# A second buffer for Strassen's raw weights, and spectral rows split in place, in a state-space and feed-forward kernel

## The chip, the core and the metric

The kernel runs on one core of a Trainium2 chip. Five engines work side by side, each through its own instructions in order, and wait for each other by semaphores: TensorE (PE in the profile, its weight loads PEld) multiplies, VectorE (DVE) and ScalarE (ACT) work on elements, GpSimd (POOL) and SyncE (SP) here mostly issue transfers. Transfers between the device's memory and the core's on-chip memory run on 16 shared DMA engines; an issue stands in the queue of the engine that makes it, and what comes behind it in that queue waits as long as it does.

The metric is the time of one execution in device microseconds. A run gives one such time; a profiled run gives also the span, from its first to its last instruction.

## What is computed

Three terms are added up: the input u (2048 x 576), a state-space convolution of the normalised input, and a feed-forward block of it with SiLU between two matrices (576 x 4608 and 4608 x 576), all in fp32.

```python
xn = _layernorm(x, axis=-1)
return x + _A_ref(xn, A_A_re, ..., A_Dskip) + _B_ref(xn, B_w1, B_w2)

def _A_ref(u, ...):                  # u is xn here
    K = einsum("dn,dnl,dn->dl", Cc, exp(logdA[:, :, None] * l), dB).real
    y = irfft(rfft(pad(u)) * rfft(pad(K)))[:L]     # along the 2048 positions
    return y + u * Dskip

def _B_ref(x, w1, w2):
    return einsum("bsf,fd->bsd", silu(einsum("bsd,df->bsf", x, w1)), w2)
```

## The kernel before

**Numbers in two parts.** Products run in fp32r, a rounded fp32. Each operand is split into a high part h (a cast on ACT) and a low part l = value - h (a subtraction on DVE), and a product is the sum of three matmuls: h by h, h by l, l by h. Splits of this kind are the commonest work of ACT and DVE: `split_w1` and `split` for w1, `split_of` (L985 the cast, L986 the subtraction) for spectral rows.

**The feed-forward part** is the main sequence (`ffn`). 2048 positions are four blocks of 512, two halves of two. w1 and w2 are cut along 4608 into 36 tiles of 128, nine chunks of four. `up` makes a 128 x 512 tile of the hidden layer (L298 to L300), with SiLU and split behind it (L306 to L308); `down` multiplies hidden tiles with w2 (L328) and adds the result into `acc` on DVE (L333). The first half and two chunks of the second half are done so. The other seven chunks of the second half, 28 tiles of 128, are done by `wino_ffn` as 14 *units* n = 4 to 17 of two tiles each, by Strassen's scheme: seven products of 256 x 256 by 512 positions (p1, p5, p6, p7, c11, c12, c2x; L453 and L459) in place of eight.

**Raw weights.** For each unit `load_w1` fetches a 576 x 256 piece of w1 from memory into a tile `w1r` of 5 x 256 numbers in each of the 128 partitions: three transfers on SP's queue (L244 to L246). `prep` then works on the tile in five steps, spread over the iteration of the unit before: the splits "c2" and "c1" (L370 the cast, L371 the subtraction), "sums" (L381 to L384, in place), and the splits "t13" and "t24". A split's results, `w1h` and `w1l`, are what PE multiplies. The tile w1r is in a pool with one buffer (`wp`), so a unit can be fetched only when the last split of the one before, its t24, has read the tile. The call for unit n+2 stands at the end of iteration n, where t24 of unit n+1 has just been put in line. The last unit, 17, is left out of that row: `tail` asks for it, into a pool of the tail (`yp`) that lies where the spectral tiles were.

**The w2 tiles of these units** come from a buffer in memory where their parts were stored before (L482, POOL's queue, tile w).

**The convolution** is the side sequence (`side`), woven into the main one by `weave`, step for step. `kgen` makes the kernel K from tables (L795 to L897), `spread` makes the first stage of the transform of u; both leave rows in memory, d1u and d1k. `spectral` then runs 32 steps k. A step fetches a row block of each (`raw`, L935, tiles ur and kr, one buffer each, SP's queue), splits both (`split_of`, L985 and L986, tiles uh, ul, kh, kl, two buffers each), multiplies them with transform matrices (L994, banks pu and pk), multiplies the two spectra on ACT and DVE (L920 to L929), and in its second part splits the result y, transforms it (pb, L994) and copies it out (L952) to d2 (L953, POOL's queue). All three banks come from one pool of three PSUM buffers, so a product has to wait until ACT's copies (L920 to L923, L952) or DVE's products have emptied the bank used three products before. ur and kr are used again as soon as their split is done; uh and ul when PE is through with the step two before.

**The tail** (`tail`) fetches d2 (L1001, tiles ys) and makes the last transform (L1013), which is added into the output.

**The order** of instructions on each engine is fixed when the program is built: a scheduler takes them in the order of the text, with priorities, and places each by a simulated time line. `issue_after` (through `behind`) keeps one behind another.

Of the kernel before, what the change touches and what calls it, by code (L numbers as in the profile page):

```python
# [10 lines left out]
F32 = mybir.dt.float32  # L11
# [6 lines left out]
P = 128  # L18
L = 2048
D = 576  # L20
# [21 lines left out]
def kernel(  # L42
# [186 lines left out]
    def ffn():  # L229
# [4 lines left out]
        R1, R2 = {}, {}  # L234
        begun = {}

        def load_w1(half, c, t, pool=None):

            f = c * FT + t
            first = half == 0 and c == 0  # L240
            r1 = (pool or (pa if first and t else w1x if t and w1x else wp)).tile([P, 5, 2 * P], F32, tag="w1r", name="w1r", bufs=1)
            fs = slice(f * P, (f + 2) * P)
            eng = nc.gpsimd if first and t == 0 else nc.sync
            eng.dma_start(r1[:, 0:4, :], w1[0:512, fs].rearrange("(k p) f -> p k f", p=P))  # L244
            eng.dma_start(r1[0:64, 4, :], w1[512:576, fs])
            pins["load"] = eng.dma_start(r1[64:128, 4, :], w1[512:576, fs]).ins  # L246
            R1[half, c, t] = r1
# [188 lines left out]
    def wino_ffn(load_w1, prep, WT, first, end, W2, before, down):  # L436

        ps_a = ps1.tile([P, 512], F32, tag="ps1", name="pa")
        ps_c = ps1.tile([P, 512], F32, tag="ps1", name="pc")
        A, A22, S1, S2, S3, S4, x40, x41, d4 = wino["x"]  # L440
        nc.tensor.matmul(ps_a, x40[:, :P], x40, start=True, stop=True)
        G = {}

        def unit(name, n, a):
            h, l = WT[name, n]
            return h[:, a:a + 2], l[:, a:a + 2]

        def prod(dst, w, x, start=False, stop=False):
            (wh, wl), (xh, xl) = w, x
            n = 0  # L450
            for a, v in ((wh, xh), (wh, xl), (wl, xh)):
                for kt in range(2):
                    pins["pe"] = nc.tensor.matmul(dst, a[:, kt], v[:, kt], start=start and n == 0, stop=stop and n == 5,  # L453
                                                  skip_group_check=True).ins
                    n += 1

        def rest(dst, name, n, at, x4, stop=True):
            for i in range(2):
                pins["pe"] = nc.tensor.matmul(dst, WT[name, n][i][:, at], x4, start=False, stop=stop and i == 1,  # L459
                                              skip_group_check=True).ins  # L460

        def gate(src, b, f):
            gf = gp.tile([P, 512], F32, tag="gf", name="gf", bufs=2)
            spare = len(G) % 6 == 5
            gh, gl = ((wino["pool"] if spare else gp).tile([P, 512], F32R, tag=n, name=n) for n in ("gh", "gl"))
            G[b, f] = gh, gl
            with tc.high_priority():
                nc.scalar.activation(gf, src, AF.Silu)
                pins["gh"] = nc.scalar.copy(gh, gf).ins  # L469
                pins["gl"] = nc.vector.tensor_sub(gl, gf, gh).ins  # L470

        def load(n):
            if n < end - 1:
                load_w1(1, n // 2, n % 2 * 2)

        wino["last"] = lambda pool: load_w1(1, (end - 1) // 2, (end - 1) % 2 * 2, pool)

        def second(n, i):
            if n < end:
                f = 2 * n + i  # L480
                w = wp.tile([P, 2, D], F32R, tag="w2", name="w2", bufs=FT + 1)
                pins["load"] = nc.gpsimd.dma_start(w, dw2[f - WINO_C * FT]).ins  # L482
                W2[1, f // FT, f % FT] = w

        load(first + 1)
        second(first, 0)

        def downs(n):

            if n < first:  # L490
                return [lambda jj=jj: down(before, jj) for jj in range(4)]
            b = 1 - n % 2
            if n == first:
                ns = (n,)
            else:
                ns = (n - 1, n)
            return run_of(b, ns)

        def run_of(b, ns):
            fs = [2 * n + i for n in ns for i in range(2)]  # L500
            blk = (1, NCH - 1 if ns[-1] == end - 1 else WINO_C, b)
            return [lambda jj=jj: down(blk, jj, [(G[b, f], W2[1, f // FT, f % FT]) for f in fs]) for jj in range(4)]

        for n in range(first, end):
            d = downs(n - 1)
            pb = ps2.tile([P, 512], F32, tag="ps2", name="pb2")
            f5 = wino["pool"].tile([P, 512], F32, tag="f5", name="f5", bufs=1)
            units = {k: unit(*k) for k in (("c1", n, 0), ("c1", n, 2), ("t13", n, 0), ("t13", n, 2),
                                           ("t24", n, 0), ("t24", n, 2), ("c2", n, 0))}

            def p1():
                prod(pb, units["c1", n, 0], A[0], start=True)
                with tc.high_priority():
                    nc.scalar.copy(ps_a, pb)

            def p5():
                prod(ps_c, units["t13", n, 0], S1, start=True)
                rest(ps_c, "c2", n, 2, x41)
                with tc.high_priority():
                    nc.scalar.copy(f5, ps_c)  # L520

            def p6():
                prod(pb, units["t24", n, 0], S2)
                with tc.high_priority():
                    nc.vector.tensor_add(ps_c, pb, f5)

            def p7():
                prod(pb, units["t13", n, 2], S3)
                with tc.high_priority():
                    nc.vector.tensor_add(f5, pb, f5)  # L530

            def c11():
                prod(ps_a, units["c1", n, 2], A[1])
                rest(ps_a, "c1", n, 4, x40)
                gate(ps_a, 1, 2 * n)

            def c12():
                prod(ps_c, units["c2", n, 0], S4)
                rest(ps_c, "c2", n, 2, d4)
                gate(ps_c, 1, 2 * n + 1)  # L540

            def c2x():
                gate(f5, 0, 2 * n + 1)
                prod(pb, units["t24", n, 2], A22)
                gate(pb, 0, 2 * n)

            def c1x():
                c12()
                c11()

            def side_w(k):
                if k == 1:
                    prep(n + 1, "c2")
                elif k == 2:
                    prep(n + 1, "c1")
                    prep(n + 1, "sums")
                elif k == 3:
                    second(n, 1)
                    second(n + 1, 0)

            if n == first:
                order = ((p1, 0), (c11, 1), (2,), (p5, p6, 3), (p7,))
                ends = c12, c2x
            else:
                order = ((p1, p5), (0,), (p6, 1), (p7, 2), (3,))
                ends = (c1x, c2x) if n % 2 == 0 else (c2x, c1x)
            for steps in order:
                for f in steps:
                    if callable(f):
                        f()  # L570
                    else:
                        d[f]()
                        side_w(f)
                yield 0
            rest(pb, "c1", n, 4, x41, stop=False)
            for k, f in enumerate(ends):
                f()
                prep(n + 1, ("t13", "t24")[k])
                yield 0
            load(n + 2)  # L580
        b = 1 - (end - 1) % 2
        for f in run_of(b, (end - 2, end - 1)):
            f()
            yield 0
        for k, f in enumerate(run_of(1 - b, (end - 1,))):
            f()
            if k % 2:
                yield 0
# [311 lines left out]
    def spectral():  # L900
# [5 lines left out]
        def front(k):  # L906
            m3 = mats("m3", k, 2)
            m2 = m2s.pop(k)
            if k < 31:
                m2s[k + 1] = mats("m2", k + 1, 0)  # L910
            us, ks = (split_of(t, n) for t, n in zip(raws.pop(k), "uk"))
            if k < 31:
                raws[k + 1] = raw(k + 1)
            ka = kl.tile([P, D], F32, tag="ka", name="ka", bufs=2)
# [15 lines left out]
            return m3, ka  # L930

        def raw(k):
            t = [kl.tile([P, D], F32, tag=n + "r", name=n + "r") for n in "uk"]
            for r, d in zip(t, (d1u, d1k)):
                nc.sync.dma_start(r, d[k * P:(k + 1) * P, :])  # L935
            return t

        m2s = {0: mats("m2", 0, 0)}
# [19 lines left out]
    def tail():  # L958
# [9 lines left out]
                conv_load(j + i + AHEAD)  # L968
            store(y, j, (nc.gpsimd,), accum_op=ALU.add)

        with behind(pins["load"]):
            wino["last"](yp)
        steps = [(tail_at[0] + j * tail_at[1], conv_load, j) for j in range(AHEAD)]
        steps += [(tail_at[2] + j * tail_at[3], last, j) for j in range(0, 8, 2)]
        for at, f, j in sorted(steps, key=lambda v: v[0]):
# [2 lines left out]
                f(j)  # L978

    yss = {}  # L980

    def split_of(t, tag, bufs=2):
        h = kl.tile([P, D], F32R, tag=tag + "h", name=tag + "h", bufs=bufs)
# [38 lines left out]
    def side():  # L1022
# [38 lines left out]
        s4 = s4p.tile([P, 32], F32, name="s4")  # L1061
        nc.gpsimd.dma_start(s4, cs4)

        xp = ctx.enter_context(tc.tile_pool(name="xp", bufs=1))
        with tc.tile_pool(name="sx", bufs=1) as sx:
            for k, _ in enumerate(wino_x(sx, xp)):
# [95 lines left out]
```

## Time and profile before

| | us |
|---|---|
| median of 3 runs | 1121.45 (1119.86 to 1123.09) |
| the profiled run's own time | 1121.59 |
| its span, first to last instruction | 1119.7 |
| busy: PE, DVE, ACT, POOL | 1091.6, 950.0, 728.1, 140.5 |
| TensorE clock granted | 1.00 all through |

Lines of the profile give, for a group, its line in the kernel, engine, operation, and tiles as output<-inputs. In order of time a row gives start, duration, engine, line, operation, tiles, count, and in brackets the idle time of that engine just before and what ended it. Rows of waits give who waited for whom, the total in us, how often, and the longest. SPq is SP's queue of transfers. The matmuls' ends are modelled, so a busy PE is not PE at its peak.

### The profile page before, as it was taken

How to read it: one execution, taken by the hardware profiler on the slowest of the kernel's cores; microseconds unless marked ns; L12 is line 12 of the kernel's file. 1: busy time of each engine (PE TensorE's matmuls, PEld its weight loads, DVE VectorE, ACT ScalarE, POOL GpSimd, SP SyncE). 2: the span in 40 equal slices, each digit the busy share in tenths (PEclk: the TensorE clock that was granted, in tenths of full speed). 3: DMA queues.
4: the chain of work that ended last, by engine and by line, in shares of the span. 5: the costliest groups of instructions: out<-in, count | busy, mean ns of one | idle time of the engine just before them, and what ended most of it. 6: DMA issues, size and time to landing. Idle time of an engine off the chain costs nothing.

```text
span 1119.7 us, 23109 instructions
## 1 busy us (share of the span) xinstructions
PE 1091.6 (97%) x9101; PEld 987.6 (88%) x9101; DVE 950.0 (85%) x1615; ACT 728.1 (65%) x1285; POOL 140.5 (13%) x244
## 2 busy tenths in 40 slices
PE   6998999999999999999999999999999999999998
PEld 5997989889988899898899988899989998999787
DVE  6698899999999999999999978988878888886333
ACT  4665455776777766676667645877767877785330
POOL 1022100000000000000330001112212112111220
PEclk9999999999999999999999999999999999999999
DMA  9455632436353536356964235456455565543985
GB/s 272 141 156 177 194 124 82 144 85 176 105 154 128 150 108 172 120 138 236 237 190 92 72 65 183 133 175 178 140 165 178 163 187 157 167 157 116 247 200 139
DMA packets 161870, 173.68 MB, mean 155 GB/s; under 512 B 88497, under 2 KB 127425, under 8 KB 161121
## 3 DMA queue, kind: packets, MB, share of 16 engines
q1 hardware_dynamic: 137200, 106.75, 34.5%
q0 software_dynamic: 23888, 63.67, 19.2%
q10 hardware_dynamic: 672, 1.77, 0.7%
q8 instruction: 72, 1.18, 0.4%
q14 instruction: 38, 0.30, 0.1%
HBM read 109.64 MB, written 62.60 MB: 154 GB/s over the span
## 4 chain that ended last, share of the span: by engine, by line
PE 70%; DVE 10%; DMA 9%; ACT 5%; issue 4%; SPq 1%; POOL 1%; ACTq 0%; DVEq 0%; POOLq 0%
PE po L328 30%; PE ph L298 16%; PE pb L453 5%; PE kp L866 3%; DMA w<-dw 2%; PE pc L453 2%; DMA w1r<-in_B_w_dram 2%; PE pb L994 2%; PE pu L994 2%; PE pk L994 2%; PE ph L299 1%; PE ph L300 1%; PE z L881 1%; PE pa L453 1%; DMA w2r<-in_B_w_dram 1%
## 5 line engine op out<-in xcount | busy, mean ns | idle before, releaser
L328 PE MATMUL po<-w,gh 128*128 128x288 f32 x2304 | 475.1, 297 | 6.2 <-ACT w L284 2.1
L328 PEld LDWEIGHTS po<-w,gh 128*128 128x128 f32 x2304 | 376.5, 188 | 22.1 <-DMA w<-dw 2.7
L328 PE MATMUL po<-w,gl 128*128 128x288 f32 x1152 | 334.9, 296 | 0.6 <-DVE gl L308 0.6
L328 PEld LDWEIGHTS po<-w,gl 128*128 128x128 f32 x1152 | 215.2, 188 | 2.6 <-DVE gl L308 0.9
L333 DVE TENSOR_TENSOR acc<-po,acc 128x288 f32<-128x288 f32 x296 | 130.3, 452 | 59.7 <-PE po L328 58.6
L298 PE MATMUL ph<-xh,w1h 128*128 128x512 f32 (+1 forms) x368 | 99.1, 388 | 0.9 <-ACT xh L123 0.7
L298 PE MATMUL ph<-xl,w1h 128*128 128x512 f32 (+1 forms) x368 | 98.5, 386 | 0.0
L298 PE MATMUL ph<-xh,w1l 128*128 128x512 f32 (+1 forms) x368 | 97.9, 383 | 0.0
L306 ACT ACTIVATE gf<-ph 128x512 f32<-128x512 f32 (+1 forms) x92 | 53.3, 579 | 60.4 <-PE ph L300 41.8
L298 PEld LDWEIGHTS ph<-xl,w1h 128*128 128x128 f32 x368 | 67.6, 191 | 12.8
L298 PEld LDWEIGHTS ph<-xh,w1l 128*128 128x128 f32 x368 | 66.6, 189 | 11.7
L298 PEld LDWEIGHTS ph<-xh,w1h 128*128 128x128 f32 x368 | 65.2, 191 | 11.2 <-ACT xh L123 1.0
L157 POOL DMA_DIRECT2D d1u<-u x32 | 17.5, 547 | 405.8 <-ACT u L156 404.5
L825 ACT ACTIVATE c<-th,magic 128x1040 f32<-128x1040 f32 x36 | 42.0, 1168 | 40.2 <-DVE C L846 28.0
L307 ACT CAST gh<-gf 128x512 fp32r<-128x512 f32 (+1 forms) x92 | 55.3, 602 | 15.5 <-PE po L328 14.5
L903 POOL DMA_DIRECT2D m<-in_cm_dram x64 | 33.9, 531 | 250.8 <-PE pu L994 147.1
L308 DVE TENSOR_TENSOR gl<-gf,gh 128x512 fp32r<-128x512 f32 (+1 forms) x92 | 60.7, 662 | 3.5 <-ACT gh L307 3.3
L827 ACT ACTIVATE c<-th 128x1040 f32<-128x1040 f32 x36 | 38.7, 1076 | 33.7 <-DVE th L826 33.6
L845 DVE TENSOR_TENSOR S<-th,C 128x1024 f32<-128x1024 f32 x36 | 44.0, 1222 | 12.1 <-ACT th L828 12.0
L470 DVE TENSOR_TENSOR gl<-gf,gh 128x512 fp32r<-128x512 f32 x56 | 38.0, 688 | 11.9 <-ACT gh L469 11.6
L370 ACT CAST w1h<-w1r 128x512 fp32r<-128x512 f32 (+2 forms) x56 | 34.6, 621 | 20.3 <-DMA w1r<-in_B_w_dram 14.6
L826 DVE SCALAR_TENSOR_TENSOR th<-c,th 128x1040 f32<-128x1040 f32 x36 | 44.5, 1237 | 0.7 <-ACT c L825 0.5
(271 smaller groups left out, 2384.5 us busy)
## 6 DMA issues: line engine op xcount, KB each, us to landing
w1r<-in_B_w_dram SPq DMA_DIRECT2D x35, 512.0 KB, 4.2
dw<-w SPq DMA_DIRECT2D x28, 576.0 KB, 4.5
w<-dw POOLq DMA_DIRECT2D x28, 576.0 KB, 6.6
w2r<-in_B_w_dram SPq DMA_DIRECT2D x44, 288.0 KB, 5.0
d1u<-u POOLq DMA_DIRECT2D x32, 288.0 KB, 2.7
d1k<-stage SPq DMA_DIRECT2D x18, 512.0 KB, 7.3
ur<-d1u SPq DMA_DIRECT2D x32, 288.0 KB, 3.3
kr<-d1k SPq DMA_DIRECT2D x32, 288.0 KB, 2.8
```

Of the source, the lines that this page charges most:

```text
L298: nc.tensor.matmul(ph, w[:, kt, :], v[:, kt, a:e], start=n + kt == 0, stop=False)
L306: nc.scalar.activation(gf, ph, AF.Silu)
L307: pins["gh"] = nc.scalar.copy(gh, gf).ins
L308: pins["gl"] = nc.vector.tensor_sub(gl, gf, gh).ins
L328: pins["pe"] = nc.tensor.matmul(po[:, :HD], gs[g][:, js], ws[:, w, hs], start=n == 0 and j not in begun, stop=n == 3 * len(terms) - 1, ski ...
L333: nc.vector.tensor_add(acc[j][:, hs], po[:, :HD], acc[j][:, hs])
L453: pins["pe"] = nc.tensor.matmul(dst, a[:, kt], v[:, kt], start=start and n == 0, stop=stop and n == 5, skip_group_check=True).ins
L825: nc.scalar.activation(c65, th, AF.Identity, bias=magic)
L826: nc.vector.scalar_tensor_tensor(th, c65, MAGIC, th, op0=ALU.subtract, op1=ALU.subtract)
L827: nc.scalar.activation(c65, th, AF.Abs)
L845: nc.vector.tensor_mul(ov3, t[:, :, 0:64].rearrange("n d (x y) -> n d x y", y=32), mv3)
L994: nc.tensor.matmul(dst, st, mv[:, hs], start=n == 0, stop=n == 3 * len(terms) - 1)
```

## The change

Three things are changed. A second pool of one buffer, `w1y`, is opened after `kgen`; `w1x` names it, and `load_w1` then takes it for every odd unit (t is 2), `wp` for every even one. The call for unit n+2 moves from the end of iteration n to its start, and unit 17 is asked for like the others; the tail's own call is gone. To make room (w1y takes 5 x 256 x 4 = 5120 bytes in a partition), the tiles ur and kr (2 x 576 x 4 = 4608 bytes) are gone: `raw` fetches the rows into the tiles ul and kl, two buffers each, and the new `split_here` casts from there to the high part and subtracts in place. `split_of` stays for y.

```diff
--- before.py
+++ after.py
@@ -234,11 +234,11 @@
         R1, R2 = {}, {}
         begun = {}
 
-        def load_w1(half, c, t, pool=None):
+        def load_w1(half, c, t):
 
             f = c * FT + t
             first = half == 0 and c == 0
-            r1 = (pool or (pa if first and t else w1x if t and w1x else wp)).tile([P, 5, 2 * P], F32, tag="w1r", name="w1r", bufs=1)
+            r1 = (pa if first and t else w1x if t and w1x else wp).tile([P, 5, 2 * P], F32, tag="w1r", name="w1r", bufs=1)
             fs = slice(f * P, (f + 2) * P)
             eng = nc.gpsimd if first and t == 0 else nc.sync
             eng.dma_start(r1[:, 0:4, :], w1[0:512, fs].rearrange("(k p) f -> p k f", p=P))
@@ -470,10 +470,8 @@
                 pins["gl"] = nc.vector.tensor_sub(gl, gf, gh).ins
 
         def load(n):
-            if n < end - 1:
+            if n < end:
                 load_w1(1, n // 2, n % 2 * 2)
-
-        wino["last"] = lambda pool: load_w1(1, (end - 1) // 2, (end - 1) % 2 * 2, pool)
 
         def second(n, i):
             if n < end:
@@ -502,6 +500,7 @@
             return [lambda jj=jj: down(blk, jj, [(G[b, f], W2[1, f // FT, f % FT]) for f in fs]) for jj in range(4)]
 
         for n in range(first, end):
+            load(n + 2)
             d = downs(n - 1)
             pb = ps2.tile([P, 512], F32, tag="ps2", name="pb2")
             f5 = wino["pool"].tile([P, 512], F32, tag="f5", name="f5", bufs=1)
@@ -577,7 +576,6 @@
                 f()
                 prep(n + 1, ("t13", "t24")[k])
                 yield 0
-            load(n + 2)
         b = 1 - (end - 1) % 2
         for f in run_of(b, (end - 2, end - 1)):
             f()
@@ -908,7 +906,7 @@
             m2 = m2s.pop(k)
             if k < 31:
                 m2s[k + 1] = mats("m2", k + 1, 0)
-            us, ks = (split_of(t, n) for t, n in zip(raws.pop(k), "uk"))
+            us, ks = (split_here(t, n) for t, n in zip(raws.pop(k), "uk"))
             if k < 31:
                 raws[k + 1] = raw(k + 1)
             ka = kl.tile([P, D], F32, tag="ka", name="ka", bufs=2)
@@ -930,9 +928,9 @@
             return m3, ka
 
         def raw(k):
-            t = [kl.tile([P, D], F32, tag=n + "r", name=n + "r") for n in "uk"]
+            t = [kl.tile([P, D], F32R, tag=n + "l", name=n + "l", bufs=2) for n in "uk"]
             for r, d in zip(t, (d1u, d1k)):
-                nc.sync.dma_start(r, d[k * P:(k + 1) * P, :])
+                nc.sync.dma_start(r.bitcast(F32), d[k * P:(k + 1) * P, :])
             return t
 
         m2s = {0: mats("m2", 0, 0)}
@@ -968,8 +966,6 @@
                 conv_load(j + i + AHEAD)
             store(y, j, (nc.gpsimd,), accum_op=ALU.add)
 
-        with behind(pins["load"]):
-            wino["last"](yp)
         steps = [(tail_at[0] + j * tail_at[1], conv_load, j) for j in range(AHEAD)]
         steps += [(tail_at[2] + j * tail_at[3], last, j) for j in range(0, 8, 2)]
         for at, f, j in sorted(steps, key=lambda v: v[0]):
@@ -978,6 +974,12 @@
                 f(j)
 
     yss = {}
+
+    def split_here(l, tag):
+        h = kl.tile([P, D], F32R, tag=tag + "h", name=tag + "h", bufs=2)
+        nc.scalar.copy(h, l.bitcast(F32))
+        nc.vector.tensor_sub(l, l.bitcast(F32), h)
+        return h, l
 
     def split_of(t, tag, bufs=2):
         h = kl.tile([P, D], F32R, tag=tag + "h", name=tag + "h", bufs=bufs)
@@ -1061,6 +1063,7 @@
         s4 = s4p.tile([P, 32], F32, name="s4")
         nc.gpsimd.dma_start(s4, cs4)
 
+        w1x = ctx.enter_context(tc.tile_pool(name="w1y", bufs=1))
         xp = ctx.enter_context(tc.tile_pool(name="xp", bufs=1))
         with tc.tile_pool(name="sx", bufs=1) as sx:
             for k, _ in enumerate(wino_x(sx, xp)):
```

## The prediction

> **What bounds the kernel now.** I read the page's shares first, then busy time by stage, then what PE and ACT waited for in the stages the change touches, then single stretches in order of time.
>
> ```profile
> span 1119.7 us, 23109 instructions
> PE 1091.6 (97%) x9101; PEld 987.6 (88%) x9101; DVE 950.0 (85%) x1615; ACT 728.1 (65%) x1285; POOL 140.5 (13%) x244
> 640.00:690.00 50.00, 48.39 (x415) 43.40 (x415) 41.52 (x64) 24.17 (x40) 5.98 (x11) 1.00 0.38 94
> 690.00:1010.00 320.00, 315.32 (x1982) 290.73 (x1981) 273.95 (x528) 252.82 (x542) 57.60 (x108) 1.00 0.56 167
> 1010.00:1080.00 70.00, 68.15 (x498) 58.56 (x498) 31.12 (x60) 27.37 (x60) 12.84 (x18) 1.00 0.78 191
> 1080.00:1120.00 40.00, 35.71 (x340) 31.33 (x338) 12.35 (x25) 4.48 (x8) 3.71 (x5) 1.00 0.63 149
> ```
>
> The columns after each stretch are its length, then the busy time of PE, PEld, DVE, ACT and POOL, then the granted clock (1.00), the DMA share and GB/s. PE is busy nearly all the time. The Strassen units start near 640 us, spectral steps run from 680 to 1010 us, and both edits lie behind 640 us; the order of instructions ahead of that is the same in both programs. From 640 to 1080 us PE is idle for 1.61 + 4.68 + 1.85 = 8.14 us, and the edits remove no PE work. That idle time is therefore all that they can win: no time under 1121.59 - 8.14 = 1113.45 us can come from them. The 4.29 us without PE in the last stretch are mostly the last additions and stores, which stay.
>
> What PE waited for from 640 us on, the four longest sums (us in total, times, longest):
>
> ```profile
> PE po L328 <- DMA w<-dw: 1.7, 2, 1.0
> PE pu L994 <- ACT kb L923: 1.3, 1, 1.3
> PE py L1013 <- DMA ys<-d: 1.1, 1, 1.1
> PE po L328 <- DVE acc L333: 1.1, 1, 1.1
> ```
>
> None of them names w1r, the raw weights that the change is about. ACT does wait for them, and what stands behind it reaches PE. ACT's waits from 690 to 1010 us, then one case in order of time (start, duration, instruction, idle before it):
>
> ```profile
> ACT w1h L370 <- DMA w1r<-in_B_w_dram: 13.4, 7, 4.2
> ACT uh L985 <- DMA ur<-d1u: 2.2, 2, 1.6
> ...
> 820.05 0.38 SPq L244 DMA_DIRECT2D w1r<-in_B_w_dram  x1
> 827.75 0.51 ACT L370 CAST w1h<-w1r 128x384 fp32r<-128x384 f32 x1 [4.21 <-DMA w1r<-in_B_w_dram]
> 829.41 0.39 ACT L923 COPY kb<-pk 64x288 f32<-64x288 f32 x1
> 829.86 0.41 PE L994 MATMUL pu<-uh,m 128*128 128x288 f32 x1 [1.30 <-ACT kb L923]
> ...
> 836.01 0.40 PE L994 MATMUL pu<-uh,m 128*128 128x288 f32 x1 [0.26 <-DVE kb L928]
> 852.85 0.38 SPq L244 DMA_DIRECT2D w1r<-in_B_w_dram  x1
> 858.36 0.40 PE L994 MATMUL pk<-kh,m 128*128 128x288 f32 x1 [0.43 <-ACT yo L952]
> ```
>
> The load was asked for at 820 us, just when the one buffer came free; ACT reached the first cast of that unit at 823.5 and stood 4.21 us. Four copies out of PSUM stood behind it, the bank that they empty was the one PE wanted, and PE lost 1.30 us, then 0.26 us while ACT and DVE caught up. At 858 us the same happened once more, 0.43 us through the copy to yo. So 13.4 us of waiting on ACT cost PE 1.30 + 0.26 + 0.43 = 1.99 us: 0.149 us for each.
>
> **The change part by part.** *Two buffers for w1r.* The ask for unit n+2 moves from the end of iteration n to its start, into the buffer whose last reader was the split of unit n, one iteration earlier. Each ask has a whole iteration more (32.8 us, from the ask at 820.05 to the next at 852.85), against 7.7 us from ask to cast in the case above. The cadence on the queue stays: one ask for each unit, at the moment a t24 split is done, only for the unit after. ACT's wait goes whole, and PE wins 1.99 us. The same splits, sums and casts run, none longer.
>
> *The new pool's first load.*
>
> ```profile
> 647.76 0.69 DVE L846 SCALAR_TENSOR_TENSOR C<-c,C 128x512 f32<-128x512 f32 x1
> 658.71 3.62 SPq L894 DMA_DIRECT2D d1k<-stage  x2
> ```
>
> The pool lies where the tables of kgen lay. In the order of SP's queue unit 5 now stands ahead of the last d1k<-stage stores and waits for those tables' last use, on DVE, over by 648.5 us; ten microseconds before the stores were issued. Unit 6 takes its old place, behind those stores and ahead of the first spectral rows. The same bytes stand before these as now: 0 us, covered by the ten microseconds; without them the stores and the first step would shift by that difference.
>
> *The last unit leaves the tail.*
>
> ```profile
> w1r<-in_B_w_dram SPq DMA_DIRECT2D x35, 512.0 KB, 4.2
> w1r<-in_B_w_dram SPq DMA_DIRECT2D x70, 64.0 KB, 4.1
> ...
> 1011.83 0.38 SPq L244 DMA_DIRECT2D w1r<-in_B_w_dram  x1
> 1028.64 0.39 SPq L244 DMA_DIRECT2D w1r<-in_B_w_dram  x1
> 1030.28 64.55 SPq L1001 DMA_DIRECT2D ys<-d  x32
> ...
> 1042.65 1.19 PE L1013 MATMUL py<-ys,s 64*32 64x288 f32 x20 [1.11 <-DMA ys<-d]
> ```
>
> Unit 17 was asked for only when the spectral tiles were free, ahead of the ys loads. Now unit 17 is asked for at the place of unit 16 (1011.8 us), and ys moves up by 1030.28 - 1028.64 = 1.64 us; besides, one transfer of 512 KB and two of 64 KB less stand before it on the DMA engines, 3.4 us at the 191 GB/s of the stretch from 1010 to 1080 us. PE's 1.11 us of wait goes, even if PE comes there 1.99 us sooner (3.10 us are needed, 5.0 us are won). Sum so far: 1.99 + 1.11 = 3.10 us.
>
> *Spectral rows in place.* The cast on ACT and the subtraction on DVE keep shape and count; only the source buffer changes. What changes is when a row may be fetched. Before, ur and kr were free as soon as their split was done. Now the fetch writes the tile ul or kl of two steps back, so SP waits for PE's last product with it. Behind that on SP stand the other row and, every third step, the three transfers of a w1r ask, which have an iteration to spare. Landing times, and step 8 in order of time:
>
> ```profile
> L935 SPq DMA_DIRECT2D ur<-d1u x32: 319/320/559, 679.1 to 991.4; - x32
> DMA to landing us min/median/max: 2.6/3.3/9.1
> L935 SPq DMA_DIRECT2D kr<-d1k x32: 319/320/531, 679.5 to 989.2; - x32
> DMA to landing us min/median/max: 2.6/2.8/8.5
> ...
> 747.12 0.32 SPq L935 DMA_DIRECT2D ur<-d1u  x1
> 755.53 0.30 PE L994 MATMUL pu<-ul,m 128*128 128x288 f32 x1
> 755.67 0.29 PE L994 MATMUL pu<-uh,m 128*128 128x288 f32 x1
> 756.16 0.68 ACT L985 CAST uh<-ur 128x576 fp32r<-128x576 f32 x1
> 770.98 0.29 PE L994 MATMUL pu<-uh,m 128*128 128x288 f32 x1
> ```
>
> The row for step 8 was asked for nine microseconds before its cast, and the cast itself waited for the high part of step 6 to be free: PE's last product with that ends at 755.96, the cast starts 0.2 us later. In the changed program the ask stands where the cast stood: data at 755.96 + 3.3 = 759.3 us, at worst 765.1. PE uses it first at 770.98, so the data themselves are never late. The price is ACT's place in line. I counted PE's new order at 0.13 us for a product of 288 columns (755.53 to 755.67) and about 0.23 us for one of 512. There the cast of u mostly stands 1.2 to 1.9 us behind that release, some 1.5 us sooner than the median row lands, in all 30 steps that can wait; in nine of them (6, 8, 9, 10, 13, 16, 20, 22, 30) the next copy that empties a bank for PE is due 2.0 to 2.6 us after the release, in the others after 3.2 us or more. How much delay PE takes there:
>
> ```profile
> w<-dw POOLq DMA_DIRECT2D x28, 576.0 KB, 6.6
> ...
> 759.45 0.51 ACT L370 CAST w1h<-w1r 128x384 fp32r<-128x384 f32 x1 [2.31 <-DMA w1r<-in_B_w_dram]
> 761.98 0.40 ACT L923 COPY kb<-pk 64x288 f32<-64x288 f32 x1
> 765.28 0.30 PE L994 MATMUL pu<-uh,m 128*128 128x288 f32 x1
> ```
>
> The first row is the slow neighbour on the DMA engines: the w2 tiles of a unit, two loads of 576 KB at a time. Below it ACT stood 2.31 us for w1r, and still kb ended 2.9 us before PE took the bank again. A delay of 1.5 us mostly fits into that. Bounds for the new waits: 0 if all fit; 30 steps of 1.5 us at 0.149 give 6.7 us, and the same for k (2.8 - 1.8 = 1.0 us each) another 4.5, together 11.2 us. I take the nine close places: 9 x 1.5 x 0.149 = 2.0 us, nearer to nothing because the row above shows 2.9 us of room.
>
> The Trainium skill (SBUF — State Buffer, "The DMA setup-cost knee") gives a transfer a fixed 2 us or so and bytes over 436 GB/s on top. For a row of 288 KB that makes 2.7 us, an estimate. The k rows agree (median 2.8 us), the u rows do not when other loads run (up to 9.1 us). By the page each wait would be 0.9 us, the nine would cost 1.2 us and the sum would end near 1119.6 us.
>
> Sum against the profiled run: 1121.59 - 3.10 + 2.0 = 1120.5 us. That run stands 0.14 us above the median of 1121.45, so 1120.4 us as a median.
>
> **The rivals.** *Slower: the wait for w1r is replaced by one for spectral rows in every step.* Place: the cast of u on ACT, 30 times, where the fetch starts only after PE. Price: 30 x 1.5 x 0.149 = 6.7 us, less 3.10, +3.6: 1125.0 us as a median; with the k rows too, 1129.5 us. It decides from 3.10 / 0.149 = 21 us of new waiting on ACT, 0.7 us in a step; the median landing makes 1.5 us. For it: SP can no longer run ahead of PE, and the slow u landings come when the 576 KB loads of w stand in front. Against it: a wait puts ACT later, which shortens the next one, and the 2.9 us of room.
>
> *Faster: the rows fit everywhere.* All 3.10 us stay won, 1118.4 us as a median, and where ACT and DVE run with more room, some of the other 8.14 - 3.10 = 5.0 us may go too; half of it gives 1115.8 us. For it: the small waits cluster behind ACT's stalls. Against it: the waits for w (1.7 us) and for the additions into acc (1.1 us) have other causes.
>
> *No change in effect: PE, earlier by 2 us, meets the next thing.* The w loads wait for PE itself and then land; a PE that comes sooner waits longer for them. The 1.99 us go into those waits, the new ones are none: 1121.59 - 1.11 = 1120.5 us, 1120.3 as a median. The order of engines is also redone behind 640 us, which can move single waits of about 1 us either way.
>
> **How the numbers follow.** A difference under 0.3% (3.4 us) can't be told from none here. The forecast and the third rival have 0.42 together; both lie within it. The slower rival has 0.33, the faster 0.25 (its lower part, beyond 3.4 us). Faster is held down since the waits that I can name give only 3.10 us; slower is held up since the shorter lead is in every step, while the wait removed showed in two. The range reaches from 1115.5 (the faster rival's half) to 1129 us (rows of both kinds waiting); the forecast's own is 1118 to 1123 us.
>
> **What would show it.** ACT's wait for w1r gone from 690 to 1010 us; a new row of ACT waits, uh (and kh) for the rows from d1u and d1k, some 14 us by my sum, over 45 us by the slower rival, near 0 by the faster. The stall of 1.30 us on pu and that of 1.11 us on py gone; unit 17's load before 1020 us. PE's idle time from 690 to 1010 us at about 4.7 us if I am right, over 8 us in the slower case, under 2.7 in the faster. Wrong in kind would be: time lost before 640 us or behind 1080 us, or a longer cast or subtraction than now.

## The result and the profile after

| | before | after |
|---|---|---|
| median, five runs each | 1121.17 us (1119.86 to 1123.09) | 1115.44 us (1112.82 to 1116.70) |
| the profiled run | 1121.59 us | 1115.58 us |

The ratio is 0.9951 with a 95% interval of 0.9935 to 0.9968: faster by 0.49%; the medians lie 5.7 us apart. The forecast was 1120.4 us and no difference that can be told. The time lies at the lower end of the range: 0.06 us under it as a time, just inside it as a ratio, since the median of the kernel before was 1121.17 us here and 1121.45 us when the range was set. It is below even the faster rival's lower figure of 1115.8 us.

The page of the changed kernel, and its busy time by stage (length; PE, PEld, DVE, ACT, POOL; granted clock, DMA share, GB/s):

```profile
span 1113.8 us, 23080 instructions
PE 1090.6 (98%) x9101; PEld 987.0 (89%) x9101; DVE 950.6 (85%) x1615; ACT 725.8 (65%) x1285; POOL 140.5 (13%) x244
640.00:690.00 50.00, 48.39 (x416) 43.45 (x415) 39.80 (x62) 24.82 (x41) 5.72 (x10) 1.00 0.45 119
690.00:1010.00 320.00, 317.62 (x2001) 293.72 (x2000) 279.16 (x538) 253.26 (x548) 57.63 (x108) 1.00 0.55 166
1010.00:1080.00 70.00, 70.00 (x525) 59.27 (x523) 27.82 (x52) 23.62 (x51) 15.88 (x22) 1.00 0.76 180
```

PE does the same work (1090.6 us against 1091.6). Its idle time fell from 4.68 to 2.38 us in the spectral stage and from 1.85 to 0.00 from 1010 to 1080 us. The stretch from 640 to 690 us is as it was. These two steps make 4.2 us of the 6.0 between the profiled runs. The rest lies ahead of 640 us, where both programs are the same: line L441, the start of the Strassen part, begins at 660.2 us instead of 661.9. That 1.7 us is taken for chance between two executions: over the twelve traces of this case PE's idle time ahead of 640 us ranges from 12.7 to 16.0 us, and the two of the kernel before alone have 16.0 and 14.4.

What PE waited for behind 640 us in the changed kernel, and ACT's longest waits from 690 to 1010 us (total, times, longest):

```profile
PE po L328 <- DMA w<-dw: 1.8, 2, 1.3
PE po L328 <- DVE acc L333: 1.1, 1, 1.1
PE pk L996 <- ACT yo L950: 0.7, 1, 0.7
```

```profile
ACT kh L980 <- DMA kl<-d1k: 17.7, 16, 3.0
ACT uh L980 <- DMA ul<-d1u: 17.0, 18, 2.9
ACT yh L987 <- DVE ka L927: 4.5, 7, 1.8
```

PE's stalls of 1.30 us on pu and of 1.11 us on py are gone, and so is ACT's wait for w1r. ACT now waits 34.7 us for spectral rows. In the kernel before it waited longest for DVE instead, 24.7 us where it is now 4.5:

```profile
ACT yh L985 <- DVE ka L929: 24.7, 14, 3.0
```

The new waits largely took the place of old ones: ACT's time without work in this stage is 320 - 252.8 = 67.2 us before and 320 - 253.3 = 66.7 us after. The stretch of step 8 shows what they cost. First the changed kernel: a row of ACT in order of time, then the busy time of that stretch, PE first. Then the kernel before, in the stretch where ACT stood 4.21 us for w1r:

```profile
762.76 0.68 ACT L980 CAST kh<-kl 128x576 fp32r<-128x576 f32 x1 [2.98 <-DMA kl<-d1k]
755.00:770.00 15.00, 15.00 (x99) 14.06 (x98) 13.90 (x28) 11.56 (x27) 2.16 (x4) 1.00 0.52 161
```

```profile
820.00:835.00 15.00, 13.70 (x90) 12.59 (x89) 10.31 (x21) 7.68 (x18) 2.13 (x4) 1.00 0.45 139
```

ACT stands 2.98 us for a row and PE is busy for all 15 us. With 4.21 us PE lost 1.30. At the tail, SP's queue and PE's first product with ys in the changed kernel:

```profile
1006.35 0.38 SPq L244 DMA_DIRECT2D w1r<-in_B_w_dram  x1
1023.19 36.88 SPq L1003 DMA_DIRECT2D ys<-d  x24
1036.19 1.20 PE L1015 MATMUL py<-ys,s 64*32 64x288 f32 x24
```

Unit 17 is asked for at 1006.4 us (before: 1028.6), ys from 1023.2 us on (before: 1030.3), and PE finds ys there without a wait although it comes 4.7 us earlier (before, its first product with ys was at 1040.87 us, and the one that waited for the next ys at 1042.65).

### The profile page after: what moved, and what is told of

Same layout as the page of the kernel before. It is cut to its first block, busy times and chain, and to the rows that moved or that the text cites. A ratio compares the mean times of both kernels' runs of the same rounds, so it can differ in the third digit from the quotient of the medians.

```text
span 1113.8 us, 23080 instructions
## 1 busy us (share of the span) xinstructions
PE 1090.6 (98%) x9101; PEld 987.0 (89%) x9101; DVE 950.6 (85%) x1615; ACT 725.8 (65%) x1285; POOL 140.5 (13%) x244
## 4 chain that ended last, share of the span: by engine, by line
PE 83%; DVE 7%; DMA 5%; ACT 2%; issue 1%; POOL 0%; SPq 0%; DVEq 0%; ACTq 0%; POOLq 0%
PE po L328 35%; PE ph L298 19%; PE pb L453 6%; PE pc L453 3%; PE kp L864 3%; PE pu L996 2%; PE pk L996 2%; PE pb L996 2%; PE pa L453 2%; PE ph L299 2%; PE ph L300 2%; DMA w<-dw 1%; PE z L879 1%; DMA w1r<-in_B_w_dram 1%; PE pc L459 1%
## 5 line engine op out<-in xcount | busy, mean ns | idle before, releaser
L807 DVE TENSOR_TENSOR th<-vt,fT 128x1040 f32<-128x1040 f32 x36 | 44.4, 1235 | 0.0
```

The costliest lines, as they stand in the source:

```text
L807: nc.vector.tensor_mul(split(th), row(vt[:, 0:65], 65), col(fT, i, 65))
```

## The experiments

Each kernel's ratio is against the kernel before on the same chip; "idle" is PE's idle time in a stretch of the trace, its length less the busy time.

**The rows alone.** One buffer for w1r and the tail as before; only the rows are fetched into ul and kl and split there.

```diff
-    t = [kl.tile([P, D], F32, tag=n + "r", name=n + "r") for n in "uk"]
+    t = [kl.tile([P, D], F32R, tag=n + "l", name=n + "l", bufs=2) for n in "uk"]
-        nc.sync.dma_start(r, d[k * P:(k + 1) * P, :])
+        nc.sync.dma_start(r.bitcast(F32), d[k * P:(k + 1) * P, :])
...
-    us, ks = (split_of(t, n) for t, n in zip(raws.pop(k), "uk"))
+    us, ks = (split_here(t, n) for t, n in zip(raws.pop(k), "uk"))
```

> The kernel before with the spectral rows fetched into ul and kl and split in place, nothing else; one w1r buffer, unit 17 asked for in the tail. Theory (the row part is free, the gain comes from the w1r asks): time as before, 1120 to 1122 us; ACT waits some 30 to 35 us for rows from 690 to 1010 us and still 10 us or more for w1r; PE idle there about 4.7 us, 1010 to 1080 about 1.9 us. Rival A (waits on ACT cost PE 0.149 us each, as in the prediction): 35 us of row waits add 5 us, 1125 us or more. Rival B (the gain came from the rows or from any new order of instructions): 1116 to 1118 us.

Measured: 1119.08 us (12 runs), ratio 0.9984 (0.9969 to 0.9999), between the theory and rival B. The spectral stage and ACT's waits in it:

```profile
690.00:1010.00 320.00, 317.28 (x2005) 293.54 (x2004) 277.27 (x537) 253.54 (x546) 57.06 (x107) 1.00 0.56 163
ACT uh L984 <- DMA ul<-d1u: 16.0, 16, 3.7
ACT w1h L370 <- DMA w1r<-in_B_w_dram: 8.2, 8, 3.2
```

The part that I had charged with +2.0 us lowers PE's idle time there from 4.68 to 2.72 us, with one buffer for w1r and 8.2 us of waiting for it. The waits for rows are 16.0 us for u and 3.1 us for k, less than the 30 to 35 us that I expected. The cast that stalled PE, and the transfers asked for ahead of it on SP's queue, first in the kernel before as it ran once more on a chip of the experiments, then with the rows alone; the last line of each is the time from the ask for w1r to its landing (least, median, most of one):

```profile
816.29 0.32 SPq L935 DMA_DIRECT2D kr<-d1k  x1
817.85 0.38 SPq L244 DMA_DIRECT2D w1r<-in_B_w_dram  x1
825.84 0.51 ACT L370 CAST w1h<-w1r 128x384 fp32r<-128x384 f32 x1 [4.48 <-DMA w1r<-in_B_w_dram]
827.95 0.40 PE L994 MATMUL pu<-uh,m 128*128 128x288 f32 x1 [1.58 <-ACT kb L923]
DMA to landing us min/median/max: 6.8/6.8/6.8
```

```profile
817.95 0.38 SPq L244 DMA_DIRECT2D w1r<-in_B_w_dram  x1
820.11 0.33 SPq L935 DMA_DIRECT2D kl<-d1k  x1
823.43 0.51 ACT L370 CAST w1h<-w1r 128x384 fp32r<-128x384 f32 x1 [0.18 <-DMA w1r<-in_B_w_dram]
DMA to landing us min/median/max: 4.0/4.0/4.0
```

The ask for w1r goes out at the same time. In the kernel before a row of k stands 1.6 us ahead of it, and the load lands 6.8 us later (6.5 in the profiled run of the prediction). With the rows in place that row has to wait for PE and is asked for 2.2 us behind w1r, which lands in 4.0 us. ACT also reaches the cast 1.9 us later (825.84 - 4.48 against 823.43 - 0.18). Both together take the wait from 4.48 to 0.18 us, with the one old buffer. That the row ahead makes the load slow is read from the two traces, not tried by itself. Nor is the row's place told apart here from the other changes in the order of instructions that come with it. The tail of the same trace, PE in order of time and two stretches (the clock stands third from the end):

```profile
1032.33 0.53 PE L328 MATMUL po<-w,gh 128*128 128x288 f32 x2 [0.96 <-DMA w<-dw]
1035.94 1.19 PE L1019 MATMUL py<-ys,s 64*32 64x288 f32 x20 [1.81 <-DMA ys<-d]
1038.04 1.06 PE L453 MATMUL pb<-s2l,w1h 128*128 128x512 f32 x2
...
1044.47 0.63 PE L453 MATMUL pa<-xl,w1h 128*128 128x512 f32 x2
```

```profile
1035.00:1040.00 5.00, 4.06 (x32) 1.80 (x32) 0.00 (x0) 1.10 (x3) 0.00 (x0) 0.71 1.09 225
1040.00:1045.00 5.00, 5.00 (x23) 4.48 (x20) 1.16 (x2) 0.40 (x1) 3.22 (x4) 0.60 1.08 224
```

PE, sooner at the tail, waits 1.81 us for ys, and behind that wait the granted clock falls: a pair of products takes 1.06 us where it takes 0.63 at full clock. By the clock the two stretches lose 5 x 0.29 + 5 x 0.40 = 3.5 us, an estimate, about twice the longer wait itself. The 12 runs divide by the clock: five with a mean clock of 1.000 took 1113.96 to 1117.06 us, seven with 0.998 or less 1118.99 to 1122.36. The five have a median of 1115.36 us, and on the same chip the kernel before at full clock had 1118.83 (five runs).

**The calls late.** Both buffers, but the ask at its old place in the text.

```diff
         for n in range(first, end):
-            load(n + 2)
...
                 yield 0
+            load(n + 2)
```

> The changed kernel with the call for unit n+2 put back to the end of iteration n; two w1r buffers, rows in place and unit 17's place in the row stay. Theory: ACT waits for w1r again (8 us or more from 690 to 1010 us), PE idle there goes from 2.4 to 4 us or more, the tail keeps its gain (idle 1010 to 1080 us under 0.5 us): 1117 to 1119 us. Rival (the lead is worth nothing, the order of instructions or the rows made the gain): 1114 to 1116.5 us.

Measured: 1115.37 us, ratio 0.9959 (0.9945 to 0.9972), idle 1.62 us in the spectral stage, no wait of ACT for w1r, and unit 17 asked for at 1003.1 us. The rival came true. Moving the call does nothing by itself: with a second buffer the asks go out at the same times from either place in the text. The three of its five runs at full clock have a median of 1115.37 us, the same as the rows alone at full clock on this chip. So what the second buffer and the earlier unit 17 add shows here only in runs whose clock falls without them.

**The rows twice.** The changed kernel with each row fetched twice into the same tile, so that the second landing counts.

```diff
+                for _ in range(2):
+                    nc.sync.dma_start(r.bitcast(F32), d[k * P:(k + 1) * P, :])
```

> The changed kernel with each spectral row fetched twice in a row into the same tile, so that the second transfer waits for the first: 2.9 to 3.4 us more from ask to data, and twice the row traffic. Theory (ACT has some 2.9 us of room before a bank is late for PE, a wait beyond it costs PE in full): ACT's wait for a row goes from about 1 us to 3 or 4 us in most steps, past the room in many of the 30 steps: PE idle from 690 to 1010 us rises from 2.4 to 10 us or more, 1122 us or more. Rival (ACT's place is never what PE waits for): PE idle there under 4 us, 1114 to 1118 us.

Measured: 1144.27 us, ratio 1.0221 (1.0197 to 1.0245). ACT's waits, PE's, and the stage:

```profile
ACT kh L981 <- DMA kl<-d1k: 43.7, 19, 5.1
ACT uh L981 <- DMA ul<-d1u: 19.9, 19, 2.3
```

```profile
PE pu L997 <- ACT kb L921: 3.5, 5, 1.2
PE pu L997 <- ACT yo L951: 3.2, 4, 1.8
690.00:1010.00 320.00, 304.15 (x1866) 274.35 (x1865) 258.23 (x496) 233.26 (x505) 53.50 (x100) 0.99 0.70 207
```

The longest wait is now 5.1 us, and PE waits for copies out of PSUM again, idle 15.85 us. ACT's waits for rows grew by 63.6 - 34.7 = 28.9 us and PE's idle time by 13.5: the mechanism of the slower rival is real, but it begins beyond the waits that the change makes. It is not the whole of the 25.4 us by which the span grew (1113.8 to 1139.2): PE's busy time grew by 9.0 us as well (1090.6 to 1099.6), and why is open. The extra traffic (207 GB/s against 166) is part of this run too.

**The changed kernel once more.**

> The changed kernel once more, for the spread of a single trace. If the 1.4 us that PE idled less ahead of 640 us, where both programs are the same, were chance, PE idle from 0 to 640 us lies between 14.5 and 16.5 us here too, with no order between kernels; from 690 to 1010 us it is again 2 to 3 us, from 1010 to 1080 us under 0.5 us.

Measured: 1111.72 us, one run. ACT waits 35.9 us for rows, the longest 3.4, and PE is idle 1.01 us in the spectral stage and 0.00 from 1010 to 1080 us. Ahead of 640 us it is idle 13.5 us, less than the 14.5 to 16.5 that I expected of chance.

**ys ahead of unit 17.** The kernel before, with unit 17 asked for behind the first twelve ys loads.

```diff
-        with behind(pins["load"]):
-            wino["last"](yp)
...
+        steps += [(tail_at[0] + AHEAD * tail_at[1], lambda j: wino["last"](yp), 0)]
```

> The kernel before with one thing moved: in the tail unit 17 is asked for behind the first twelve ys loads in place of ahead of them. Theory (most of the gain is the tail: PE's wait for ys, and a dip of the granted clock that follows such a wait in most runs): the wait of 1.1 us on py and the dip are gone, mean clock 0.999 or 1.000 in nearly all runs, 1116.5 to 1118.5 us. Rival A (the gain comes from the spectral stage, rows or buffers): 1119.5 to 1121 us. Rival B (unit 17 now comes too late for its first cast): a new wait on w1r at the end, 1121 us or more.

Measured: 1128.61 us, ratio 1.0066 (1.0049 to 1.0084). ACT's first cast of unit 17, PE's wait in the tail, and the stretch behind it:

```profile
1054.73 1.14 ACT L370 CAST w1h<-w1r 128x384 fp32r<-128x384 f32 x2 [11.77 <-DMA w1r<-in_B_w_dram]
1056.25 0.85 PE L328 MATMUL po<-w,gh 128*128 128x288 f32 x2 [7.84 <-DVE acc L333]
1055.00:1060.00 5.00, 3.75 (x14) 3.65 (x15) 4.62 (x10) 0.87 (x2) 0.00 (x0) 0.50 0.43 88
```

The wait for ys is gone, and rival B came true: unit 17 goes out at 1037.6 us and lands only 16.4 us later (the median of the asks from 640 us on is 4.5). ACT stands 11.77 us for it, and PE 7.84 us. PE's row names DVE's additions as the releaser; the load of unit 17 is what moved.

**The rows and ys first.** Both edits above together, one buffer.

> The kernel before with the spectral rows in place and unit 17 asked for behind the first ys loads, still one w1r buffer and the late asks. Theory (rows and tail make the gain, the second buffer none): as the changed kernel, 1114.5 to 1116.5 us, though ACT still waits 8 us or so for w1r from 690 to 1010 us. Rival (the second buffer is worth the 2 us of the prediction): 1117 to 1119 us.

Measured: 1126.49 us, ratio 1.0050 (1.0032 to 1.0067). I missed here: unit 17 goes out at 1032.0 us, lands 17.4 us later, and ACT stands 12.70 us for it.

```profile
1051.67 0.85 PE L328 MATMUL po<-w,gh 128*128 128x288 f32 x2 [8.80 <-DVE acc L333]
```

In these traces with one buffer either ys or unit 17 is late in the tail, whichever stands second.

**ys late.** The changed kernel with the first pair of ys loads made three times, so that only the wait for ys comes back.

```diff
-            for h in range(2):
+            for h in (0, 1) * (3 if j == 0 else 1):
```

> The changed kernel with the first pair of ys loads made three times over into the same tile, so that the first product py has its data some 5 to 10 us later. Theory (a wait of PE near 2 us in the tail, among the small matmuls of py, drops the granted clock for some 10 us and costs about 3.5 us beside itself): PE waits 2 to 6 us for ys, then a stretch of 5 to 10 us with a granted clock of 0.6 to 0.75, mean clock 0.995 to 0.998, 1118 to 1124 us. Rival (the dips have nothing to do with that wait): the wait alone, clock as in the changed kernel (0.999 or 1.000), 1116.5 to 1120 us.

Measured: 1120.68 us (10 runs), ratio 0.9995 (0.9981 to 1.0009). The wait, and the stretch behind it:

```profile
1044.18 2.15 PE L1015 MATMUL py<-ys,s 64*32 64x288 f32 x32 [4.38 <-DMA ys<-d]
1045.00:1050.00 5.00, 5.00 (x42) 3.82 (x27) 0.46 (x1) 1.31 (x4) 2.14 (x4) 0.72 1.06 223
```

This one wait gives back nearly all that the change won, though it is four times as long as the 1.11 us of the kernel before. The spectral stage stays at 1.63 us idle, and none of the ten runs has a mean clock above 0.998.

**The kernel before once more.**

> The kernel before once more, for the spread of a single trace. Theory: PE idle 690 to 1010 us 4 to 5.5 us and 1010 to 1080 us near 1.9 us as in the first trace; if its mean clock is 0.998 or less, the dip lies within 10 us behind the wait of py for ys. Rival: the dip lies elsewhere, or PE idle 690 to 1010 us is as low as 2.7 us here too (then rows_only won nothing there).

Measured: 1119.9 us, one run; idle 5.82 us in the spectral stage, 1.89 from 1010 to 1080 us, and no fall of the clock behind its 1.0 us wait for ys.

**The second buffer for unit 17 alone.** Rows in place, the calls at the end of an iteration; units 5 to 16 share the one old buffer.

```diff
-    r1 = (... w1x if t and w1x else wp).tile(...)
+    r1 = (... w1x if t and w1x and ((half, c) < (1, WINO_C) or c == 8) else wp).tile(...)
```

> Rows in place, calls at the end of an iteration, and the second buffer taken by unit 17 alone; units 5 to 16 share the old buffer as before. Theory (the rest of the gain lies in the tail): ACT waits for w1r again, 7 to 10 us from 690 to 1010 us, PE's idle time there stays at 1.5 to 3 us, unit 17 is asked for before 1010 us, PE has no wait for ys and no dip of the granted clock from 1010 to 1080 us; median 1114.5 to 1117 us, within 0.15% of the kernel with both buffers for all units. Rival (the second buffer pays in the spectral stage, where it ends ACT's wait for w1r): PE idle over 3.5 us from 690 to 1010 us, median 1118 to 1120 us, as with the rows in place alone.

**Both buffers beside it**, the kernel with the calls late again, on the same chip.

> Both buffers for all units, the calls at the end of an iteration, once more on the chip of the run above, so that the two can be compared. Theory and rival both: no wait of ACT for w1r, no wait of PE for ys, PE idle from 690 to 1010 us 1 to 2.5 us, median 1113 to 1117 us. If it and the run above differ by less than 0.15%, the second buffer is worth nothing beyond the tail; if this one is over 0.2% faster, it is worth something in the spectral stage too.

Measured: 1115.45 us, ratio 0.9952 (0.9933 to 0.9970), for unit 17 alone; 1115.27 us, ratio 0.9943 (0.9925 to 0.9960), for both buffers. First the kernel with unit 17 alone, its wait for w1r and two stages; then the spectral stage with both buffers:

```profile
ACT w1h L370 <- DMA w1r<-in_B_w_dram: 7.1, 6, 3.0
690.00:1010.00 320.00, 316.94 (x2002) 293.29 (x2001) 277.22 (x535) 254.59 (x548) 57.60 (x108) 1.00 0.57 167
1010.00:1080.00 70.00, 69.63 (x511) 60.09 (x510) 28.81 (x55) 23.37 (x50) 15.96 (x22) 1.00 0.81 190
```

```profile
690.00:1010.00 320.00, 316.58 (x1993) 292.85 (x1993) 278.08 (x536) 251.85 (x545) 57.23 (x108) 1.00 0.56 165
```

ACT waits 7.1 us for w1r again. The longest of these waits, 2.99 us, is followed by stalls of PE of 0.23 and 0.47 us, but on the whole nothing is lost that can be told: the medians lie 0.2 us apart, PE's idle time in the spectral stage is 3.06 us against 3.42 (1.84 us of which is one wait for w; I had expected 1 to 2.5). With a buffer to itself unit 17 is asked for at 638.3 us, before all other units but 4. Once the rows are in place, a gain from the second buffer shows for one load only, that of unit 17.

A second buffer without the rows in place wasn't tried (the room for it comes from ur and kr), nor was the old call for unit 17 in the changed kernel.

## What the prediction had right and what it had wrong, point by point

**The time.** The forecast missed by 4.9 us and said that no difference could be told, where one can. That the range reached down to the measured time is owed to the faster rival, to which I gave 0.25, the smallest of the three chances; it is luck and no merit of the sum.

**The bound** holds. From 640 to 1080 us PE's idle time fell from 8.14 to 1.61 + 2.38 + 0.00 = 3.99 us, and nothing won in the profiled run lies outside it but the 1.7 us ahead of 640 us. It was drawn at full clock, and left out what a fall of the clock costs in other runs.

**Two buffers, -1.99 us: the wait went, the price and the cause were wrong.** ACT's wait for w1r is gone, as said. But the 1.99 us were not won by the second buffer: with the rows alone the stall goes too, and with unit 17 alone in the new buffer ACT waits 7.1 us at no loss that can be told. And 0.149 us for each us of waiting, the mean over seven waits, is not how the price goes. In the three traces with the old rows the longest wait of ACT for w1r and PE's stall behind it were 4.21 and 1.30, 4.48 and 1.58, 4.84 and 1.94 us: each time the stall is the wait less 2.9 us. (The third pair is from the kernel with ys ahead of unit 17, whose spectral stage is that of before.) At the other cast that stalled PE, that of 858 us in the prediction, the pairs are 1.70 and 0.43, 2.21 and 0.95, 2.02 and 0.77 us: there it is the wait less 1.3. In the second trace of the kernel before:

```profile
856.09 0.51 ACT L370 CAST w1h<-w1r 128x384 fp32r<-128x384 f32 x1 [2.21 <-DMA w1r<-in_B_w_dram]
856.96 0.40 PE L994 MATMUL pk<-kh,m 128*128 128x288 f32 x1 [0.95 <-ACT yo L952]
```

So each place has a room of its own, and PE pays for the excess over it.

**Rows in place, +2.0 us: this is the step that failed.** The waits are there, and longer than I worked out: 34.7 us against some 14, and above the 21 us from which the slower rival was to decide. I priced nine of them at the mean rate. Their longest is 3.0 us, and where they fall PE has room for them (waits of up to 3.4 us passed in the second trace of the changed kernel). The row of 2.9 us of room stood in the prediction, but only as a leaning toward the lower bound, where the sum needed the room of each place as a limit to each wait. Waits past their room do cost, as the rows fetched twice show (5.1 us, PE's idle time 13.5 us up), and one row wait did with the rows alone:

```profile
788.43 0.67 ACT L984 CAST uh<-ul 128x576 fp32r<-128x576 f32 x1 [3.67 <-DMA ul<-d1u]
789.45 0.40 PE L1000 MATMUL pk<-kh,m 128*128 128x288 f32 x1 [1.23 <-ACT yo L952]
```

The same place gave 3.62 and 1.17, and 3.63 and 1.17 us, in the two other kernels whose units share the old buffer beside rows in place: a room of 2.4 to 2.5 us. In place of a loss there was a gain: the traces with the old rows have 4.68, 5.82 and 4.25 us of idle time in the spectral stage, the eight with the rows in place and fetched once 1.01 to 3.42, 2.3 in the mean. One source of it was shown above, the fetch of k that moved behind the ask for w1r; the rest I can't name wait by wait, and whether it comes from the rows themselves or from the new order of instructions that they bring was not told apart.

**The last unit out of the tail, -1.11 us: the mechanism was right, the size too small.** The ask for ys moves up by 7.1 us (1030.3 to 1023.2) and PE by 4.7, so the 1.11 + 4.7 = 5.8 us that were needed are there. The term itself was mis-sized: the trace of before showed a wait of 1.11 us at full clock, and I took that for its whole price. A stretch of 70 us had 1.85 us of idle time to win, not 1.11. And a wait at this place can cost clock behind it, 3.5 us in the trace with the rows alone. The two traces of the kernel before show no such fall, so that it happens there is argued, from the runs: of its 45 beside the experiments, 23 have a mean clock of 0.998 or less (median 1121.4 us) and 15 have 1.000 (median 1119.6 us). Of its own twelve runs the kernel with the rows alone, which has the old tail, has seven with 0.998 or less. Of the 16 runs of the changed kernel and its form with the late calls, one has 0.998.

**The first load of the new pool, 0 us,** holds: from 640 to 690 us PE is busy 48.39 us in both. Unit 5 goes out at 637.8 us, earlier than the 648.5 us that I took for its release.

**The sum as it should have been:** 4.9 - 2.3 = 2.6 us in the spectral stage and 1.9 us of idle time in the tail make 4.5 us. Runs at full clock differ by 1119.55 - 1115.27 = 4.3 us (15 of before, 11 of the changed kernel and its form with the late calls). That the remaining 1.3 us or so of the 5.7 come from the clock is likely, not shown. The split between the two parts is not settled either: the rows alone at full clock are 3.5 us faster than the kernel before on their chip and no slower than the kernel with both buffers and the late calls, in five and three runs.

**The rivals.** *Faster* came true in the bounds I set for it (idle time under 2.7 us, none of the stalls left), but for another reason than ACT's freedom from w1r. *Slower* falls by its own mark: 34.7 us of new waiting, and no loss. *No change in effect* falls too: PE came sooner and met little. From the Trainium skill (SBUF — State Buffer, "The DMA setup-cost knee") I had worked out 2.7 us for a row, an estimate; the rows in the changed kernel landed in a median of 2.9 (ul) and 3.4 us (kl):

```profile
ul<-d1u SPq DMA_DIRECT2D x32, 288.0 KB, 2.9
kl<-d1k SPq DMA_DIRECT2D x32, 288.0 KB, 3.4
```

That landing time was near enough; the 1.2 us of cost that I worked out by it failed through the same price.

## What to carry to other kernels

Price a wait on an engine off the bound by its excess over the room that the bound engine has there, wait by wait and place by place, and not by a mean rate: here 35 us of waits of at most 3 us cost nothing that shows, one of 4.2 us cost 1.3, and one of 2.2 us, at a place with less room, 0.95. When the matmul engine's waits near the end are counted, look at the granted clock behind each, and ask whether it comes back in every run. Of a change in two parts, test each part alone: here the part made only to find room won the spectral stage, and the extra buffer showed a gain for a single load.

## What the runs showed of the hardware

The clock fell behind short waits. The Trainium skill (TensorE: Matmul & The Clock Gate, "Part 1: The HAM clock gate") has the clock at half rate after an idle window of about 3.4 us, and back after a busy one. The waits of 4.38 and 7.84 us agree with it (0.72 and 0.50 in the five microseconds behind them). In the trace with the rows alone the clock fell to 0.71 and 0.60 behind waits of only 0.96 and 1.81 us, 3.6 us apart with some small products of 64 x 32 between and after them, while in the kernel before a single wait of 1.11 us before such products left 1.00. The stretch ahead of the fall:

```profile
1030.00:1035.00 5.00, 3.16 (x20) 2.14 (x18) 0.92 (x2) 0.59 (x1) 0.00 (x0) 1.00 1.14 262
```

There PE was busy for 3.16 of 5 us. Whether the share of busy time, the size of the products or the moment of the wait decides was not tried.
